# Twelve dummy matmuls and a fill of four in the head of a fused state-space and feed-forward layer, its four parameter vectors transposed together

## The chip, the cores and the metric

The kernel runs on one core of one Trainium2 chip. The metric is the device time of one execution in microseconds (us), lower is better. The time before is 183.56 us, the median of three runs (183.51 to 183.78).

## The reference, cut to what matters

```python
xn = _layernorm(x, axis=-1)              # x: (1, 2048, 512) bf16
# A: a diagonal state space model over 512 complex states
dt = jnp.exp(log_dt); Lam_bar = jnp.exp(dt * Lam)
B_bar = ((Lam_bar - 1.0) / Lam)[:, None] * Bmat
Bu = jnp.einsum("bld,pd->blp", xn + 0j, B_bar)
for t in range(L): h = Lam_bar * h + Bu[:, t, :]; hs.append(h)
A = 2.0 * jnp.einsum("blp,dp->bld", hseq, Cmat).real + xn * Dskip
# B: a gated feed-forward layer, F = 1376
B = (_silu(xn @ w_gate) * (xn @ w_up)) @ w_down
return x + A + B
```

Four parameter vectors of 512 numbers (`Lambda_re`, `Lambda_im`, `log_dt`, `Dskip`) steer part A.

## The kernel before, in words

The 2048 rows are 16 tiles of 128, worked in four chunks of 512 columns of the transposed input. Per chunk TensorE computes the gate and up projections (11 tiles of F each, `ffn_gate`, `ffn_up`, both by `ffn_mm`, L733), the projection into the state space (`ssm_b_chunk`, L814), the down projection (`dc_chunk`, L902) and the way back out of the states (L918). The scalar engine (ACT) evacuates PSUM and applies silu, the vector engine (DVE) normalizes, scans over time and adds up, GpSimd (POOL) computes a few powers. Results of TensorE go through eight PSUM banks; `next_bank` deals them in turn from a counter and passes over a bank that TensorE has written and for which no reader has been recorded yet. A matmul into a bank waits for the last reader of what the bank held.

Each step is recorded as a task with its reads and writes. TensorE's and the sync engine's tasks run in the order of recording; the tasks of DVE, ACT and POOL are ordered by a list scheduler from estimated times, and then run in that order, each engine by itself and strictly in turn.

The head, which the change touches, is recorded so:

- `pe_warm(9)` (L466): nine matmuls of 512 columns on a constant operand of ones. Their result is not used.
- `ln_head`: statistics and normalization of the first four tiles on DVE, with POOL for the reciprocal root (`rstd`). The normalized tile a is `xn0` to `xn3`.
- `ffn_gate_quarters` (L760): gate tiles 0 to 5 of the first chunk in quarters of 128 columns, so that each quarter can start when its row tile is transposed. Tiles 0 to 2 (A) need only the first weight load `ld_wgA`, tiles 3 to 5 (B) need `ld_wg0`. The transposes (L572) of row tile a are called `xT`a here and their evacuation by ACT (L578) `xTev`a. Between the first tile's transposes and its matmuls stands `pe_fill(3)` (L474): three dummies of 128 columns.
- `params_t` (L483, L486): the parameter vectors, loaded as rows by ACT's DMA queue, are transposed by TensorE and copied to SBUF by DVE: vectors 0 to 2 (`parT0`) after the first quarter, vector 3 (`Dskip`, `parT3`) before the last quarter. With vector 3 come four diagonal matrices `diagD` on DVE (L490).
- From the copied parameters POOL computes `dt` (L635), DVE `thn` (L637) and a row of small operations, ACT the phase table `tm0` (L684), DVE its reduction `tt1s0`, `tzs0` (L686, L688), ACT the sine table `sinT0` (L690). In ACT's order `xTev2`, `tm0`, `xTev3`, `tm1`, `sinT0` stand ahead of the six `silu` (L786) that evacuate the six gate tiles, `silu0_0` first.
- Then come the up projections of the same tiles, `mm_u0_0` to `mm_u0_5` (L733), and the rest of the kernel.

Of the kernel before, what the change touches and what calls it, by code (L numbers as in the profile page):

```python
# [18 lines left out]
    ffn_evac_act=(True, True, True, True),  # L19
    ln_norm_act=(False, False, True, True),  # L20
    wprep_act=True,
    warm=9,
    prio_tab=0.0,
    prio_par=0.0,
    rs_dve_from=8,
# [226 lines left out]
def bass_parallel_sum__ssm_conv_s5__swiglu_ffn__prompt_kernel(  # L252
# [30 lines left out]
    g = _Graph()  # L283
    es = ExitStack()
    with es:
# [53 lines left out]
        def one_c(n):  # L339
            return nc.const_aps.tensor(1.0, [128, n], B16)  # L340
# [19 lines left out]
        pbank = _PB()  # L360
# [15 lines left out]
        def next_bank():  # L376
            for _ in range(NB):
                b = bank_ctr[0] % NB
                bank_ctr[0] += 1
                if not _bank_live(b):  # L380
                    return b
            raise AssertionError("all PSUM banks live")
# [3 lines left out]
        def BK(b):  # L386
            return [("bk", b, 0), ("bk", b, 1)]
# [51 lines left out]
        def loads_stage_b2():  # L439
# [14 lines left out]
              writes=[("iot",)], name="iota", est=1000)  # L454
# [4 lines left out]
              name="act_warm", est=220, prio=1e6)  # L459

        def pe_warm(n):
            bk = next_bank()

            def mm(e, bk=bk):
                for _ in range(n):
                    inst = e.matmul(pbank[:, bk, :], lhsT=one_c(128), rhs=one_c(512), start=True, stop=True)  # L466
                return inst
            g.add("pe", mm, writes=BK(bk), name="pe_warm", est=n * 430, ninst=n)

        def pe_fill(n, bk):  # L470

            def mm(e, bk=bk):
                for _ in range(n):
                    inst = e.matmul(pbank[:, bk, 0:128], lhsT=one_c(128), rhs=one_c(128), start=True, stop=True)  # L474
                return inst
            g.add("pe", mm, writes=BK(bk), name="pe_warm_fill", est=n * 107, ninst=n)

        def params_t(ks):
            slot = next_tr()

            def tr(e, slot=slot):
                for k in ks:
                    inst = e.transpose(out=ptr[:, slot, 4 * k:4 * k + 4], in_=prow[0:4, k, :], identity=ident[0:4, 0:4])  # L483
                return inst
            g.add("pe", tr, reads=[("prow", k) for k in ks] + [("ident",)], writes=BK(slot), name="parT%d" % ks[0], est=30 * len(ks), ninst=len(ks))
            g.add("dve", lambda e, slot=slot: e.tensor_copy(out=praw[:, ks[0]:ks[-1] + 1].rearrange("p k a -> p (k a)"), in_=ptr[:, slot, 4 * ks[0]:4 * ks[-1] + 4]),  # L486
                  reads=BK(slot), writes=[("praw", k) for k in ks], name="parTev%d" % ks[0], est=80, prio=5000.0)
            if 3 in ks:
                for kt in range(KT):
                    g.add("dve", lambda e, kt=kt: e.tensor_scalar(out=diagD[:, kt, :], in0=ident[:], scalar1=praw[:, 3, kt:kt + 1], scalar2=None, op0=ALU.mult),  # L490
                          reads=[("praw", 3), ("ident",)], writes=[("diagD", kt)], name="diagD%d" % kt, est=90)
# [41 lines left out]
        def XN(c, j):  # L533
            return [("xnT", c % 2, j, 0), ("xnT", c % 2, j, 1)]
# [29 lines left out]
        def xt_tile_fine(c, a, parts=1):  # L564
            n = KT // parts
            for h in range(parts):
                slot = next_tr()
                k0 = h * n

                def tr(e, a=a, slot=slot, k0=k0):  # L570
                    for kt in range(k0, k0 + n):
                        inst = e.transpose(out=ptr[:, slot, (kt - k0) * 128:(kt - k0 + 1) * 128],  # L572
                                           in_=xn_sb[:, a % NXN, kt * 128:(kt + 1) * 128], identity=ident[:])
                    return inst
                g.add("pe", tr, reads=[("xn", a % NXN), ("ident",)], writes=BK(slot), name="xT%d_%d" % (a, h), est=n * 64, ninst=n)

                def evac(e, a=a, slot=slot, k0=k0):
                    return e.activation(out=xnT[:, c % 2, a % 4, k0:k0 + n, :],  # L578
                                        in_=ptr[:, slot, 0:n * 128].rearrange("p (k t) -> p k t", k=n), func=AF.Identity)
                g.add("act", evac, reads=BK(slot), writes=(XN(c, a % 4) if parts == 1 else [XN(c, a % 4)[h]]), name="xTev%d_%d" % (a, h), est=130 + 110 * n, prio=20000.0)  # L580
# [140 lines left out]
        def wres(nm, i):  # L721
            if nm == "wg" and i < 3:
                return ("wg", "a")
            return (nm, 0 if i < 6 else 1)
# [24 lines left out]
        def ffn_gate_quarters(c, tiles):  # L749
            xt_tile_fine(c, 4 * c, parts=2)  # L750
            banks = {i: next_bank() for i in tiles}

            def quarter(q, ts, h0, h1):
                for i in ts:
                    fs = fsz[i]
                    bk = banks[i]

                    def mm(e, bk=bk, i=i, fs=fs, q=q):
                        for kt in range(2 * h0, 2 * h1):
                            inst = e.matmul(pbank[0:fs, bk, q * 128:(q + 1) * 128], lhsT=wg[:, kt, i * 128:i * 128 + fs], rhs=xnT[:, c % 2, q, kt, :],  # L760
                                            start=(kt == 0), stop=(kt == KT - 1))
                        return inst
                    n = 2 * (h1 - h0)
                    g.add("pe", mm, reads=[wres("wg", i)] + XN(c, q)[h0:h1], writes=BK(bk), name="mm_gq%d_%d_%d_%d" % (c, i, q, h0), est=n * 62, ninst=n)

            A, B = tiles[:3], tiles[3:]
            pe_fill(3, banks[tiles[-1]])
            quarter(0, A, 0, 1)
            xt_tile_fine(c, 4 * c + 1)
            quarter(0, A, 1, 2)  # L770
            quarter(0, B, 0, 2)
            params_t([0, 1, 2])
            quarter(1, A, 0, 2)
            xt_tile_fine(c, 4 * c + 2)
            quarter(1, B, 0, 2)
            xt_tile_fine(c, 4 * c + 3)
            quarter(2, tiles, 0, 2)
            params_t([3])
            quarter(3, tiles, 0, 2)
            for i in tiles:  # L780
                fs = fsz[i]
                bk = banks[i]
                sl = gctr[0] % NG
                gctr[0] += 1
                sg_slot[(c, i)] = sl
                g.add("act", lambda e, sl=sl, bk=bk, fs=fs: e.activation(out=sg[0:fs, sl, :], in_=pbank[0:fs, bk, :], func=AF.Silu),  # L786
                      reads=BK(bk), writes=[("sg", sl)], name="silu%d_%d" % (c, i), est=490)
# [145 lines left out]
        if _CFG["warm"]:  # L933
            pe_warm(_CFG["warm"])
        ln_head()
        ffn_gate_quarters(0, [0, 1, 2, 3, 4, 5])
        params_a()
        tables()
# [98 lines left out]
```

## Time and profile before

| what | value |
|---|---|
| median of the runs | 183.56 us (183.51 to 183.78) |
| profiled execution | 184.87 us |
| its span, first to last instruction | 183.1 us |
| TensorE busy in the span | 179.2 us (98%), 939 matmuls |
| DVE busy | 166.2 us (91%) |
| ACT busy | 92.2 us (50%) |
| POOL busy | 13.1 us (7%) |
| TensorE in the chain that ended last | 95% |

The profile is one execution. The chain that ended last is followed back from the last instruction, at each step to what released it. In the timeline each row has a start, a length, an engine, a line of the kernel, the operation with what it writes and reads, and a count; in brackets stands how long the engine had been idle and what ended that. A matmul row's length ends with its last matmul's drain, so that matmuls in a stream start closer together than one lasts.

### The profile page before, as it was taken

The page shows a single profiled execution, that of the slowest core. Times are in us where ns is not written, and L with a number is a line of the kernel's source. Part 1 is how long each engine was busy: PE and PEld are TensorE (multiplying, and loading weights), DVE is VectorE, ACT ScalarE, POOL GpSimd, SP SyncE. Part 2 cuts the span into 40 slices and gives each one's busy share as a digit, 9 for nine tenths or more (in the row PEclk, how much of TensorE's full clock was granted, in tenths as well). Part 3 has the DMA queues.
Part 4 walks back from the last instruction along what each step waited for, and adds up shares of the span by engine and source line. Part 5 has one row for each costly group of instructions (what it writes and reads, how often), then busy time and mean ns, then how long its engine had stood idle before and what let it go on. Part 6 is the DMA issues. An engine that isn't in the chain of part 4 may idle for free.

```text
span 183.1 us, 2586 instructions
## 1 busy us (share of the span) xinstructions
PE 179.2 (98%) x939; PEld 88.5 (48%) x939; DVE 166.2 (91%) x360; ACT 92.2 (50%) x163; POOL 13.1 (7%) x29
## 2 busy tenths in 40 slices
PE   8899999999999999999999999999999999999994
PEld 2795444444444545444444554444444444444643
DVE  3668898999999998999999989999999999999963
ACT  3259999997799407147667471017766630000000
POOL 4340220000000005000000050000000000000000
PEclk9999999999999999999999999999999999999999
DMA  5993467669200000630000000620000000000202
GB/s 135 321 378 88 91 119 115 141 182 352 72 0 4 0 0 0 116 118 0 0 0 0 0 4 0 115 87 27 0 4 2 2 0 0 0 32 0 82 32 86
DMA packets 23404, 12.39 MB, mean 68 GB/s; under 512 B 15104, under 2 KB 23392, under 8 KB 23392
## 3 DMA queue, kind: packets, MB, share of 16 engines
q1 hardware_dynamic: 23360, 12.23, 24.7%
q8 instruction: 7, 0.11, 0.3%
q14 instruction: 5, 0.04, 0.1%
q10 hardware_dynamic: 32, 0.00, 0.0%
HBM read 6.46 MB, written 2.10 MB: 47 GB/s over the span
## 4 chain that ended last, share of the span: by engine, by line
PE 95%; DMA 2%; SPq 1%; DVE 0%; issue 0%
PE pb L733 39%; PE pb L902 21%; PE pb L918 15%; PE pb L814 15%; PE pb L760 4%; DMA wg<-in_B_w_gate_dram 2%; PE pb L905 1%; SPq L406 1%; PE pb L572 0%; DVE osb L929 0%; PE pb L483 0%
## 5 line engine op out<-in xcount | busy, mean ns | idle before, releaser
L733 PE MATMUL pb<-xnT,wu 128*128 128x512 bf16 (+1 forms) x176 | 43.7, 379 | 0.0
L902 PE MATMUL pb<-wd,hT 128*128 128x512 bf16 (+3 forms) x187 | 39.7, 367 | 0.0
L853 DVE TENSOR_TENSOR_SCAN vq<-sm,car,vq 128x512 bf16<-128x512 f32 x32 | 39.5, 1270 | 0.1
L733 PE MATMUL pb<-xnT,wg 128*128 128x512 bf16 (+1 forms) x152 | 38.4, 379 | 0.0
L798 ACT ACTIVATE uf<-pb 128x512 bf16<-128x512 f32 (+1 forms) x44 | 25.9, 605 | 17.4 <-DVE hT L800 10.2
L918 PE MATMUL pb<-W,hss 128*128 128x512 bf16 (+1 forms) x136 | 28.3, 366 | 0.0
L814 PE MATMUL pb<-xnT,BT 128*128 128x512 bf16 x128 | 28.1, 379 | 0.0
L733 PEld LDWEIGHTS pb<-xnT,wu 128*128 128x128 bf16 (+1 forms) x176 | 17.6, 100 | 20.1
L902 PEld LDWEIGHTS pb<-wd,hT 128*128 128x128 bf16 (+1 forms) x187 | 18.0, 98 | 18.5
L746 ACT ACTIVATE sg<-pb 128x512 bf16<-128x512 f32 (+1 forms) x38 | 22.6, 597 | 7.2 <-PE pb L733 6.9
L733 PEld LDWEIGHTS pb<-xnT,wg 128*128 128x128 bf16 (+1 forms) x152 | 15.3, 101 | 17.6
L800 DVE TENSOR_TENSOR hT<-sg,uf 128x512 bf16<-128x512 bf16 (+1 forms) x44 | 18.5, 420 | 2.9 <-ACT uf L798 1.2
L918 PEld LDWEIGHTS pb<-W,hss 128*128 128x128 bf16 x136 | 13.2, 98 | 13.9
L821 ACT ACTIVATE u_sb<-pb 128x512 bf16<-128x512 f32 x16 | 9.6, 597 | 20.4 <-PE pb L814 19.8
L814 PEld LDWEIGHTS pb<-xnT,BT 128*128 128x128 bf16 x128 | 12.5, 98 | 15.1
L505 POOL TENSOR_TENSOR rstd<-ve,mhalf 128x1 f32<-128x1 f32 x16 | 9.6, 618 | 92.5 <-DVE ve L503 92.5
L499 DVE BATCH_NORM_STATS2 st<-x_sb 128x6 f32<-128x512 bf16 x16 | 10.2, 681 | 2.9 <-DMA x_sb<-in_A_x_dram 2.9
L859 DVE TENSOR_TENSOR scrA<-vq,cosT 128x1024 bf16<-128x1024 bf16 x16 | 10.9, 684 | 0.0
L863 DVE TENSOR_TENSOR scrA<-vq,sin 128x1024 bf16<-128x1024 bf16 x16 | 10.9, 683 | 0.0
L847 DVE TENSOR_TENSOR scrA<-u_sb,sin 128x1024 bf16<-128x1024 bf16 x16 | 10.9, 682 | 0.0
L844 DVE TENSOR_TENSOR scrA<-u_sb,cosT 128x1024 bf16<-128x1024 bf16 x16 | 10.9, 680 | 0.0
L823 ACT ACTIVATE u_sb<-pb 128x512 bf16<-128x512 f32 x16 | 9.5, 593 | 2.3 <-PE pb L814 2.3
(72 smaller groups left out, 136.2 us busy)
## 6 DMA issues: line engine op xcount, KB each, us to landing
out_dram<-osb SPq DMA_DIRECT2D x15, 128.0 KB, 1.7
x_sb<-in_A_x_dram SPq DMA_DIRECT2D x3, 512.0 KB, 7.4
wd<-in_B_w_down_dram SPq DMA_DIRECT2D x1, 1280.0 KB, 6.9
wg<-in_B_w_gate_dram SPq DMA_DIRECT2D x2, 384.0 KB, 4.2
wu<-in_B_w_up_dram SPq DMA_DIRECT2D x1, 768.0 KB, 6.9
wg<-in_B_w_gate_dram SPq DMA_DIRECT2D x1, 608.0 KB, 8.0
wu<-in_B_w_up_dram SPq DMA_DIRECT2D x1, 608.0 KB, 9.1
x_sb<-in_A_x_dram SPq DMA_DIRECT2D x4, 128.0 KB, 2.2
```

What stands on the lines that cost most here:

```text
L733: inst = e.matmul(pbank[0:fs, bk, :].rearrange("p (j t) -> p j t", j=4), lhsT=w[:, kt, i * 128:i * 128 + fs], rhs=xnT[:, c % 2, :, kt, :], ...
L746: g.add("act", lambda e, sl=sl, bk=bk, fs=fs: e.activation(out=sg[0:fs, sl, :], in_=pbank[0:fs, bk, :], func=AF.Silu), reads=BK(bk), write ...
L798: g.add("act", lambda e, ul=ul, bk=bk, fs=fs: e.activation(out=uf[0:fs, ul, :], in_=pbank[0:fs, bk, :], func=AF.Identity), reads=BK(bk), w ...
L800: g.add("dve", lambda e, sl=sl, ul=ul, fs=fs, i=i, hb=hb: e.tensor_tensor(out=hT[0:fs, hb, i, :], in0=sg[0:fs, sl, :], in1=uf[0:fs, ul, :] ...
L814: inst = e.matmul(pbank[:, bk, :].rearrange("p (j t) -> p j t", j=4), lhsT=BT[:, ri, kt, pt * 128:(pt + 1) * 128], rhs=xnT[:, c % 2, :, kt ...
L844: g.add("dve", lambda e, sl=sl, U=U, Cb=Cb: e.tensor_tensor(out=pr2[:, sl, 0], in0=U, in1=Cb, op=ALU.mult), reads=ru + rdt, writes=[("pr", ...
L847: g.add("dve", lambda e, sl=sl, Usw=Usw, S2=S2: e.tensor_tensor(out=pr2[:, sl, 1], in0=Usw, in1=S2, op=ALU.mult), reads=ru + rdt, writes=[ ...
L853: g.add("dve", lambda e, sl=sl, ri=ri, pt=pt, rr=rr, c=c: e.tensor_tensor_scan(out=vq[:, sl, 1, ri, :], data0=rr[:, pt:pt + 1].to_broadcas ...
L859: g.add("dve", lambda e, sl=sl, Q=Q, Cb=Cb: e.tensor_tensor(out=po2[:, sl, 0], in0=Q, in1=Cb, op=ALU.mult), reads=rq + rdt, writes=[("po", ...
L863: g.add("dve", lambda e, sl=sl, Qsw=Qsw, S2sw=S2sw: e.tensor_tensor(out=po2[:, sl, 1], in0=Qsw, in1=S2sw, op=ALU.mult), reads=rq + rdt, wr ...
L902: inst = e.matmul(pbank[:, bk, 0:nc_], lhsT=hT[0:fs, hb, i, lt * 128:(lt + 1) * 128], rhs=wd[0:fs, i, c0:c0 + nc_], start=(i == 0), stop=F ...
L918: inst = e.matmul(pbank[:, bk, 0:nc_], lhsT=hss[:, hb, pt, ri, lt * 128:(lt + 1) * 128], rhs=W12[:, ri, pt, c0:c0 + nc_], start=False, sto ...
```

## The change

The stream of dummies at the start grows from nine matmuls of 512 columns to ten, and two of 128 columns follow. The fill between the first transposes and the first gate matmuls grows from three to four. The four parameter vectors are transposed in one step, where vectors 0 to 2 stood, and copied in one step; the later step for vector 3 is gone. With that one call of `next_bank` goes too, so that the banks behind it are dealt differently, and the scheduler places the `diagD` behind `xn3`.

```diff
-    warm=9,
+    warm=10,
...
                 for _ in range(n):
                     inst = e.matmul(pbank[:, bk, :], lhsT=one_c(128), rhs=one_c(512), start=True, stop=True)
+                for _ in range(2):
+                    inst = e.matmul(pbank[:, bk, 0:128], lhsT=one_c(128), rhs=one_c(128), start=True, stop=True)
                 return inst
-            g.add("pe", mm, writes=BK(bk), name="pe_warm", est=n * 430, ninst=n)
+            g.add("pe", mm, writes=BK(bk), name="pe_warm", est=n * 430 + 220, ninst=n + 2)
...
-            pe_fill(3, banks[tiles[-1]])
+            pe_fill(4, banks[tiles[-1]])
             quarter(0, A, 0, 1)
             xt_tile_fine(c, 4 * c + 1)
             quarter(0, A, 1, 2)
             quarter(0, B, 0, 2)
-            params_t([0, 1, 2])
+            params_t([0, 1, 2, 3])
             quarter(1, A, 0, 2)
             xt_tile_fine(c, 4 * c + 2)
             quarter(1, B, 0, 2)
             xt_tile_fine(c, 4 * c + 3)
             quarter(2, tiles, 0, 2)
-            params_t([3])
             quarter(3, tiles, 0, 2)
```

## The prediction, made before the changed kernel ran

> **What bounds the kernel now.** I read the chain of waits first, then the timeline of TensorE over the first 17 us, then the timeline of the other engines there. The chain, in order of time (start, us, what):
>
> ```profile
> 2.18 3.99 DMA wg<-in_B_w_gate_dram
> 6.17 0.14 issue
> 6.30 0.80 PE pb L760 x6
> ...
> 13.15 0.11 PE pb L483
> 13.26 1.45 PE pb L760 x24
> 14.70 13.81 PE pb L733 x64
> ```
>
> A load of gate weights (`ld_wgA`) lands at 6.17; from 6.30 on TensorE is the path without a break until the last tile at 180.66. The list of waits has only two for TensorE, 0.8 us at the start and 0.4 us before the first transposes, both in the head. Going through the code's dependencies with the trace's times, every later matmul group has its operands and its bank at least 5 us early, but two: `mm_b2_0_0` (0.42 us after its transposing DMA landed, which TensorE itself releases, so it moves along) and `mm_b3_0_0` (2.2 us, the same way). A us won or lost before `mm_u0_0` (the first L733, at 14.54) is therefore a us of the whole. The prediction is the new start of `mm_u0_0`.
>
> The head on TensorE (start, length, then line and count):
>
> ```profile
> 0.82 4.00 PE L466 MATMUL pb<-const-bfloat16-1.0 128*128 128x512 bf16 x9 [0.82 <-PEq L1022]
> 5.26 0.58 PE L572 MATMUL pb<-ident,xn_sb 128*128 128x128 bf16 x4 [0.44 <-DVE ve L503]
> 5.64 0.52 PE L474 MATMUL pb<-const-bfloat16-1.0 128*128 128x128 bf16 x3
> 6.30 0.80 PE L760 MATMUL pb<-xnT,wg 128*128 128x128 bf16 x6
> 6.90 0.63 PE L572 MATMUL pb<-ident,xn_sb 128*128 128x128 bf16 x4
> 7.32 2.13 PE L760 MATMUL pb<-xnT,wg 128*128 128x128 bf16 x18
> 9.38 0.23 PE L483 MATMUL pb<-ident,prow 4*128 4x4 bf16 x3
> ...
> 11.65 1.50 PE L760 MATMUL pb<-xnT,wg 128*128 128x128 bf16 x24
> 13.08 0.17 PE L483 MATMUL pb<-ident,prow 4*128 4x4 bf16 x1
> ```
>
> The same 128-column matmul comes every (2.13 - 0.31)/17 = 107 ns at 7.3 us and every (1.50 - 0.22)/23 = 56 ns at 11.7 us (0.31 and 0.22 are the length of one). The spacing changes at 10.2 us in the trace. The page's clock row shows full speed throughout, so the spacing is what must be read: TensorE runs at half rate to 10.2 us. Nine dummies at 0.427 us did not raise it; it rose 3.9 us after TensorE's last pause, the one before 6.30.
>
> The vector and scalar engines just before the gate tiles are evacuated:
>
> ```profile
> 9.66 0.17 DVE L486 COPY praw<-pb 128x12 bf16<-128x12 bf16 x1 [1.68 <-PE pb L483]
> 9.90 1.11 POOL L635 TENSOR_TENSOR sm<-ecst,praw 128x4 f32<-128x4 f32 x1 [1.52 <-DVE praw L486]
> 11.05 0.16 DVE L637 SCALAR_TENSOR_TENSOR sm<-sm,praw 128x4 f32<-128x4 f32 x1 [0.83 <-POOL sm L635]
> 12.49 0.40 DVE L686 TENSOR_SCALAR scrC<-scrC 128x512 f32<-128x512 f32 x1
> 12.92 0.69 DVE L688 SCALAR_TENSOR_TENSOR scrC<-scrC 128x512 f32<-128x512 f32 x1
> 13.65 0.63 ACT L690 ACTIVATE sin<-scrC 128x512 bf16<-128x512 f32 x1 [0.39 <-DVE scrC L688]
> 14.18 3.02 ACT L786 ACTIVATE sg<-pb 128x512 bf16<-128x512 f32 x6
> ```
>
> This second chain starts at the parameter transposes and ends in the six `silu`, which stand behind `sinT0` in ACT's queue. In the kernel before it ends just off the path: `silu0_0` finishes at 14.76 and `mm_u0_1`, which takes its bank, starts at 15.40.
>
> **The change, part by part.**
>
> *Dummies.* A tenth dummy and two short ones follow 4.19 (the ninth's start): 4.62 + 0.43 + 2 x 0.107 = 5.26, where the transposes start anyway on `xn0` (done 5.11). A fourth fill ends at 5.64 + 4 x 0.107 = 6.07, before 6.30. Cost nothing; their cover is the wait for `xn0` and for `ld_wgA`, and if either came early the dummies would cost at most 0.65 and 0.1 us. What they change is the pauses: 0.65 + 0.34 us without a running matmul (4.62 to 5.26, 5.96 to 6.30) become 0.23 us (6.07 to 6.30). By the one rise in the trace, 3.9 us after the last long pause, the clock would rise at 0.82 + 3.9 = 4.7 us; if the pause at 6.1 still spoils it, at 10.2 as now. I take the early rise. Anywhere before about 7 us gives the same sum, since the next limit is at 7.6.
>
> Against the early rise could speak that four transposes fall into that stretch. The trace's stretch before 10.2 holds four transposes (6.90), three small ones (9.38) and a 0.14 us gap, and the clock rose behind it, so by this row they don't prevent it. The Trainium skill (TensorE: Matmul & The Clock Gate, Part 4) says that transposes do not count as busy for this clock; by that the stretch with the dummies might fail as well, which is the second rival's time, 183.86.
>
> *What the faster clock meets.* The six matmuls and transposes after 6.30 speed up, but `quarter(0, B)` needs `ld_wg0`, landed at 7.59: start 7.59 + 0.14 (as behind `ld_wgA`) = 7.73. Before it was 7.96. Then at 56 ns: 12 matmuls, last one starts at 8.35; four parameter transposes (the first 0.15 behind it as at 13.08, then 0.046, 0.027, 0.027 as at 9.38), last start 8.61. Then 0.09 + 12 x 0.056 + 4 x 0.056 + 12 x 0.056 + 4 x 0.056 brings `quarter(2)` to 10.48, just when `xTev2` is done; 24 matmuls to 11.82 (`xTev3`, behind `tm0` on ACT, is done near 11.65); without the second parameter transpose (0.2 us around 13.08) 24 more to 13.16. If nothing else bound, `mm_u0_0` would start 14.54 - 13.16 = 1.38 us earlier.
>
> *The bank.* Here the joined transposes cost something. `next_bank` deals eight banks in turn. Before, `parT3` took the bank after `xT3`'s, and the counter wrapped past the six live gate banks so that `mm_u0_0` got `xT3`'s bank, free since 12.65, and `mm_u0_1` the bank of gate tile 0. Without `parT3`, `mm_u0_0` gets the bank of gate tile 0 and must wait for `silu0_0`. So the second chain becomes the path, and everything behind `mm_u0_0` in TensorE's queue waits with it. Its new times, each step by the offsets of the rows above:
> - last parameter transpose 8.61, copy 0.20 later: 8.81; POOL's `dt` 0.24 later: 9.05; `thn` 1.15 later: 10.19.
> - `thn` to `tt1s0`: 1.44 (11 small operations); the new order swaps a reciprocal for a cast, 0 to 0.1 less: 11.54 to 11.64. `tm0` on ACT, from 10.45 to 11.16, is in time.
> - `tzs0` 0.43 later, `sinT0` 0.73 after that, `silu0_0` 0.54 after that and 0.58 long: 13.82 to 13.92. `mm_u0_0` 0.10 later: 13.92 to 14.02.
>
> I take 13.97: TensorE stands idle from 13.16 to 13.97, and 14.54 - 13.97 = 0.57 us are left of the 1.38. `mm_u0_1` needs `silu0_1` 0.49 us later, while `mm_u0_0` lasts 0.86: no second wait.
>
> *diagD and the copy.* The four `diagD` move from 13.72 up behind `xn3`. They take 0.74 us (0.25 each, 0.16 apart), into the 0.83 us in which the vector engine waits for `dt`: nothing, with 0.1 to 0.25 us of room; without that cover up to 0.74. The second copy (0.15) goes. The fourth parameter vector has landed at 4.04.
>
> **Sum.** Profiled execution: 184.87 us, of which the span is 183.1; less 0.57 is 184.3. The median of the runs is 1.31 below the profiled execution; I carry the difference over: 183.56 - 0.57 = 182.99. What a measurement of this kernel can tell from no change is about 0.2%, 0.37 us, so the gain is only just above it.
>
> **Rivals.**
>
> *The clock is early already in the timed runs (slower).* The nine dummies run 3.8 us without a pause, and the rise in the trace came 3.9 us after one: a hair decides. The profiled execution is 1.31 us over the median. Were the clock full by 6.3 us in the timed runs of the kernel before, its `mm_u0_0` would start at 13.16 + 0.20 (the second transpose is still there) = 13.36, 1.18 earlier than in the profile, which is nearly that 1.31. Then the change brings only the bank wait: 13.97 - 13.36 = +0.61, 184.17. It decides once the clock rises before about 8 us without the change. Against it: profiling may lengthen a run by itself, and the three runs lie within 0.27 us. The Trainium skill (TensorE: Matmul & The Clock Gate, Part 1) says that the window runs freely and does not restart with the kernel, so the rise would differ from run to run; the trace has one execution and can't show it.
>
> *The dummies don't raise the clock.* The pause at 6.07, or operands that are all ones, spoil it, and the rise stays at 10.2. Then the second chain starts only 0.03 us later than before and loses 0 to 0.1 on the way: `mm_u0_0` at 14.79 to 14.89, +0.25 to +0.35, 183.86.
>
> *No bank wait.* If the chain to `silu0_0` ran ahead of what I add up, the limit is 13.16: 182.18. Every row of that chain speaks against it.
>
> *The new pause of 0.8 us drops the clock again.* Half a rate over another 3.9 us, the time the rise took, would cost 3.9/2 = 1.95 us more: about 184.9. For it: pauses of 1.0 us in all kept the clock down before 6.3 us. Against it: once risen, it is not seen to fall in this trace, which has no such pause behind the rise.
>
> **How the numbers follow.** Forecast 0.48; early already, or early in some runs, 0.27; clock not raised 0.14; no bank wait 0.04; clock drops 0.07. Faster by over 0.2%: four fifths of the forecast, and the 0.04: 0.42. Slower: four fifths of 0.27, the 0.07 and some of the unraised clock (its upper bound is at the edge): 0.34. The rest within: 0.24. The forecast's own range is 182.75 to 183.25 (0.25 us for the unknown order of small operations and the landings). The range for 8 in 10 takes in the early case: 182.7 to 184.25.
>
> **What would show it.** Spacing of L762 (the old L760) at 56 ns from 6.8 us or earlier, `quarter(0, B)` at 7.7; the copy of the parameters near 8.8 with one width of 16; the four `diagD` before `thn`; TensorE idle for about 0.8 us before the first L735, released by ACT; that line at 13.9 to 14.0. Wrong if 107 ns lasts to 10.2 (dummies do nothing), if no idle stands before the first up-projection (no bank wait), or if the profile shows 0.6 gained and the timed runs don't (the clock differed between them).

## The result and the profile after

The changed kernel is slower: 184.06 us median of 10 runs (183.86 to 184.71) against 183.53 us of 10 runs of the kernel before (183.25 to 183.83), ratio 1.0033, 95% interval 1.0019 to 1.0047. Yet the two profiled executions stand the other way: the span is 182.5 us after and was 183.1 us before. The profiled execution lies 0.25 us above the median of the runs after (184.31 us), and lay 1.34 us above it before (184.87 us). Both comparisons are true, and why they differ is the point of what follows.

The chain that ended last, after (start, us, what; the longest pieces):

```profile
3.19 4.50 DMA wg<-in_B_w_gate_dram
7.74 0.84 PE pb L762 x12
9.05 1.12 POOL sm L637
11.96 0.70 DVE scrC L690
12.68 0.63 ACT sin L692
13.31 0.49 ACT sg L787
13.94 13.97 PE pb L735 x64
```

TensorE is no longer the path from 6.3 us on. The path leaves it after `quarter(0, B)` and the four parameter transposes behind it (L485), goes over POOL, the vector and the scalar engine to the first silu (L787) and comes back at 13.94. The list of TensorE's waits says the same:

```profile
PE pb L466 <- PEq L1023: 0.8, 1, 0.8
PE pb L735 <- ACT sg L787: 0.6, 1, 0.6
PE pb L762 <- DMA wg<-in_B_w_gate_dram: 0.3, 1, 0.3
```

TensorE's timeline in the head:

```profile
0.82 4.42 PE L466 MATMUL pb<-const-bfloat16-1.0 128*128 128x512 bf16 x10 [0.82 <-PEq L1023]
5.04 0.42 PE L468 MATMUL pb<-const-bfloat16-1.0 128*128 128x128 bf16 x2
5.25 0.63 PE L574 MATMUL pb<-ident,xn_sb 128*128 128x128 bf16 x4
...
6.37 0.49 PE L762 MATMUL pb<-xnT,wg 128*128 128x128 bf16 x6
...
7.74 0.84 PE L762 MATMUL pb<-xnT,wg 128*128 128x128 bf16 x12 [0.31 <-DMA wg<-in_B_w_gate_dram]
8.51 0.25 PE L485 MATMUL pb<-ident,prow 4*128 4x4 bf16 x4
...
10.49 2.84 PE L762 MATMUL pb<-xnT,wg 128*128 128x128 bf16 x48
13.94 4.26 PE L735 MATMUL pb<-xnT,wu 128*128 128x512 bf16 x19 [0.61 <-ACT sg L787]
```

The dummies run into the transposes without a pause, as forecast, and six matmuls take 0.49 us at 6.37 where they took 0.80: the clock record in the trace, which lists from when to when TensorE was granted which rate, has the full rate from 6.37 us on (before: from 10.21). The time at which the full rate begins is called the rise from here on. Three rows of the chain to the silu:

```profile
8.80 0.17 DVE L488 COPY praw<-pb 128x16 bf16<-128x16 bf16 x1 [0.76 <-PE pb L485]
...
10.19 0.17 DVE L639 SCALAR_TENSOR_TENSOR sm<-sm,praw 128x4 f32<-128x4 f32 x1 [0.25 <-POOL sm L637]
...
13.22 3.02 ACT L787 ACTIVATE sg<-pb 128x512 bf16<-128x512 f32 x6
```

Added up in the prediction: copy 8.81, `thn` 10.19, `silu0_0` from 13.24 to 13.34, `mm_u0_0` at 13.97. Measured: 8.80, 10.19, 13.22, 13.94. The profile of the changed kernel is the forecast one. What was not forecast is how the timed runs stand to the first profile.

### The profile page after: what moved, and what is told of

The parts are those of the page before. It is cut to its first block, busy times and chain, and to the rows that moved or that the text cites. A ratio compares the mean times of both kernels' runs of the same rounds, so it can differ in the third digit from the quotient of the medians.

```text
span 182.5 us, 2586 instructions
## 1 busy us (share of the span) xinstructions
PE 177.8 (97%) x935; PEld 87.4 (48%) x943; DVE 165.9 (91%) x359; ACT 92.5 (51%) x163; POOL 13.1 (7%) x29
## 4 chain that ended last, share of the span: by engine, by line
PE 91%; DMA 2%; DVE 2%; SPq 1%; issue 1%; ACT 1%; POOL 1%
PE pb L735 39%; PE pb L903 21%; PE pb L815 15%; PE pb L919 15%; DMA wg<-in_B_w_gate_dram 2%; SPq L406 1%; PE pb L906 1%; POOL sm L637 1%; PE pb L762 0%; DVE scrC L690 0%; ACT sin L692 0%; ACT sg L787 0%; DVE osb L930 0%; DVE sm L611 0%; DVE scrC L688 0%
## 5 line engine op out<-in xcount | busy, mean ns | idle before, releaser
L903 PE MATMUL pb<-wd,hT 128*128 128x512 bf16 (+3 forms) x181 | 38.9, 366 | 0.3
```

What stands on the lines that cost most here:

```text
L903: inst = e.matmul(pbank[:, bk, 0:nc_], lhsT=hT[0:fs, hb, i, lt * 128:(lt + 1) * 128], rhs=wd[0:fs, i, c0:c0 + nc_], start=(i == 0), stop=F ...
```

## The experiments

Theory A: the time at which TensorE's clock rises differs from execution to execution. In most executions of the kernel before, nine dummies bring the rise before the first gate matmul; the first profile caught one of the others. Then the change has nothing to win with its dummies in the median, and pays the bank wait. Theory B: the clock rises at about 10 us in all executions of the kernel before, and the profiled one was longer for another reason. First, four kernels on one chip, which share 35 runs of the kernel before (183.51 us median).

**A second profile of the kernel before.** No edit.

> The kernel before, unchanged, for a second profile. Theory A (the clock is up early in the timed runs of the kernel before, and the first profile caught an execution in which it was late): most executions have a span near 181.8 us (183.53 less the 1.77 that lie around the span); a profile of such a one shows 128-column matmuls 56 ns apart from 6.3 us on and the first up-projection at 13.3 to 13.4. Theory B (the clock is late in all executions, the profiled one is longer for another reason): 107 ns up to about 10 us and the first up-projection near 14.5 again. Time 183.5 either way.

Measured: 183.55 us, ratio 0.9995 (0.9978 to 1.0013), spans of the 12 runs from 181.5 to 182.1 us. Its timeline:

```profile
0.82 4.00 PE L466 MATMUL pb<-const-bfloat16-1.0 128*128 128x512 bf16 x9 [0.82 <-PEq L1022]
5.34 0.50 PE L572 MATMUL pb<-ident,xn_sb 128*128 128x128 bf16 x4 [0.52 <-DVE ve L503]
...
6.29 0.50 PE L760 MATMUL pb<-xnT,wg 128*128 128x128 bf16 x6 [0.28 <-DMA wg<-in_B_w_gate_dram]
...
7.63 0.84 PE L760 MATMUL pb<-xnT,wg 128*128 128x128 bf16 x12 [0.29 <-DMA wg<-in_B_w_gate_dram]
...
13.25 4.05 PE L733 MATMUL pb<-xnT,wu 128*128 128x512 bf16 x18
```

The same program, the same dummies, but the six matmuls at 6.29 take 0.50 us (0.80 in the first profile) and the up-projection starts at 13.25 instead of 14.54, 1.29 us earlier; the spans differ by as much (181.8 and 183.1). The clock's record has the rise at 5.62 us here, and the profiled execution (183.59 us) lies 0.04 us above the median of its runs, so that it is not the profiling that lengthens an execution by 1.3 us. Theory B is out. In the kernel before, the pause between dummies and transposes (0.52 us by this profile) did not prevent the rise.

**The dummies alone.**

```diff
-            params_t([0, 1, 2, 3])
+            params_t([0, 1, 2])
...
             quarter(2, tiles, 0, 2)
+            params_t([3])
```
(against the changed kernel)

> The dummies alone (ten and two, then four), the parameter vectors transposed in two steps as before. Theory A: nothing left to win, 183.5 (-0.1 to +0.1). Theory B: the whole 1.2 us of the earlier clock without the bank wait, 182.35.

Measured: 183.54 us, ratio 0.9996 (0.9972 to 1.0020). Nothing to win, as theory A has it; its rise was at 4.65 us.

**The joined transposes alone** (`warm=9`, `pe_fill(3)`, no short dummies):

> The joined transposes alone, nine dummies and a fill of three as before. Theory A: the bank wait at full price, 13.97 instead of 13.36 for the first up-projection, +0.6: 184.1, the same as the whole change. Theory B: the chain to the first silu is late by itself, +0.25 to +0.35: 183.85.

Measured: 184.12 us, ratio 1.0032 (1.0012 to 1.0052). This part alone is as slow as the whole change.

**The whole change with the bank given back:**

```diff
             quarter(2, tiles, 0, 2)
+            next_bank()
             quarter(3, tiles, 0, 2)
```

> The whole change with one bank dealt and left unused where the second parameter transpose stood, so that the first up-projection gets the bank it had before. Theory A: the wait for the first silu goes, the removed transpose step is won: 13.16 against 13.36, -0.2: 183.3. Theory B: -1.38: 182.15. If the wait has another cause than the bank: 184.06 as in the changed kernel.

Measured: 183.18 us, ratio 0.9983 (0.9966 to 0.9999). One call that computes nothing takes 0.88 us off the changed kernel. This version and the joined transposes alone happen to start `quarter(0, B)`, which waits for `ld_wg0`, at the same time in their profiles, so that these can be laid side by side. First the joined transposes alone, then the version with the spare bank:

```profile
7.32 0.84 PE L760 MATMUL pb<-xnT,wg 128*128 128x128 bf16 x12 [0.25 <-DMA wg<-in_B_w_gate_dram]
...
13.52 3.83 PE L733 MATMUL pb<-xnT,wu 128*128 128x512 bf16 x17 [0.60 <-ACT sg L785]
```

```profile
7.32 0.84 PE L762 MATMUL pb<-xnT,wg 128*128 128x128 bf16 x12 [0.31 <-DMA wg<-in_B_w_gate_dram]
...
12.76 4.48 PE L735 MATMUL pb<-xnT,wu 128*128 128x512 bf16 x20
```

From the same 7.32 the up-projection comes 13.52 - 12.76 = 0.76 us later where it waits for the silu: that is the price of the bank.

Four more kernels, on another chip with 31 runs of the kernel before (183.52 us median), ask what holds the bank, what the dummies are worth, and whether more can be won.

**Two silu ahead of the sine table.** Banks as in the changed kernel; the tasks `sinT0` and `msinT0` get the additional order

```diff
+                      order=((silu_q[0], silu_q[1]) if pt == 0 else ())
```

> The whole change, banks dealt as in it, but on ACT the first two silu go ahead of the first sine table. If the wait before the first up-projection is for the bank of gate tile 0 and that bank is held up by the sine table ahead of it in ACT's order, the first silu ends near 13.0 instead of 13.8 and the wait goes: the first up-projection at 13.1 to 13.3, 183.2 to 183.4, like the version with the spare bank. If the bank is not what holds it, 184.06 as in the changed kernel.

Measured: 183.35 us, ratio 0.9986 (0.9970 to 1.0002); 0.7 us below the changed kernel, though `mm_u0_0` still takes the bank of gate tile 0. ACT, then TensorE, from its timeline:

```profile
12.17 3.02 ACT L789 ACTIVATE sg<-pb 128x512 bf16<-128x512 f32 x6
```

```profile
13.04 4.26 PE L735 MATMUL pb<-xnT,wu 128*128 128x512 bf16 x19
```

The silu start at 12.17 instead of 13.22, and no idle time stands before the up-projection. The added order names two silu; the scheduler put all six ahead, and the first sine table went from 12.68 to 16.46. So it is the bank, and the bank is held by ACT's order.

**No dummies at all.** `pe_warm` only takes its bank, `pe_fill` is gone, the rest as before the change.

> The kernel before without any dummies, its banks dealt as before. If the clock needs a stretch of about 3.4 us that TensorE works almost through, and such stretches lie differently in every execution, the rise comes between 8.5 and 12 us in all of them, and the first up-projection between 13.7 and 15.4: 183.9 to 185.6, median near 184.7, a wide spread. If the dummies do nothing for the timed runs (the clock is up at their start for another reason), 183.5 as before.

Measured: 184.98 us (184.34 to 185.75, 8 runs), ratio 1.0072 (1.0045 to 1.0100). Its profile has the rise at 10.22 us and the up-projection at 14.46, as in the first profile of the kernel before:

```profile
6.16 0.80 PE L755 MATMUL pb<-xnT,wg 128*128 128x128 bf16 x6 [0.35 <-ACT xnT L573]
...
14.46 2.75 PE L728 MATMUL pb<-xnT,wu 128*128 128x512 bf16 x12
```

The level is 0.3 us above what I expected, the spread of 1.4 us as expected.

**The spare bank with nine dummies** (the version with the spare bank, `warm=9`, `pe_fill(3)`, no short ones):

> The joined transposes with the spare bank, nine dummies and a fill of three as before. If the new dummies win nothing in most executions: median 183.2 as with them, and about one execution in nine near 184.4 (late clock, as 4 of 35 of the kernel before had a span of 183.1 us or more). If the new dummies carry the gain of the version with the spare bank: 183.5.

Measured: 183.34 us, ratio 0.9990 (0.9970 to 1.0009), one of 12 runs at 184.51. The median lies 0.16 above the version with the new dummies, which these runs can't tell from nothing. The late executions can be counted among those with a mean granted clock of 0.999 or more. With nine dummies (kernel before, its copy, the joined transposes with and without the spare bank) 6 of 109 executions are 1.1 us or more above their kernel's median; with the twelve and four (changed kernel, dummies alone, spare bank, silu first, and the next one) none of 58. Three more runs of the kernel before, at 185.13, 185.60 and 186.59 us, are not counted: their mean granted clock is 0.991, and the 0.9% lost are 1.65 us by themselves. So in about one execution of eighteen the new dummies may do what they were added for. This is suggested, not shown: at one in eighteen, 58 executions without a late one have a chance of about 4 in 100, none of the late ones was profiled, and the dummies alone had two executions 0.77 and 0.83 us above their median.

**Parameters transposed during the wait for `ld_wg0`** (on the version with the spare bank):

```diff
+            params_t([0, 1, 2, 3])
             quarter(0, B, 0, 2)
-            params_t([0, 1, 2, 3])
```

> The version with the spare bank, and the four parameter transposes ahead of the first quarter of gate tiles 3 to 5, into the 0.3 us in which TensorE waits for the load of their weights. They cost TensorE nothing there: first up-projection 0.3 us earlier, 182.9. If the vector engine, which now takes the parameters' copy before the last statistics, makes the third or fourth row tile late, the gain is lost: 183.2 or more.

Measured: 183.32 us, ratio 0.9979 (0.9961 to 0.9997), not the 182.9 hoped for. The transposes do fall into the gap (7.18), but a new wait takes most of the gain. ACT, then TensorE, from its timeline:

```profile
8.99 0.72 ACT L686 ACTIVATE scrC<-iot,sm 128x512 f32<-128x512 f32 x1 [1.44 <-DVE sm L639]
9.62 0.58 ACT L580 ACTIVATE xnT<-pb 128x512 bf16<-128x512 bf16 x1
```

```profile
9.81 0.39 PE L574 MATMUL pb<-ident,xn_sb 128*128 128x128 bf16 x4
10.25 2.85 PE L762 MATMUL pb<-xnT,wg 128*128 128x128 bf16 x48
```

The scheduler now puts `tm0` (L686) ahead of `xTev2` (L580) on ACT, which so ends at 10.20, and the third quarter waits for it: it starts 0.44 us after the transposes in front of it, where it starts 0.23 us after them in the version with the spare bank. No idle time stands in TensorE's row, since the transposes' drain reaches to 10.20. From the start of `quarter(0, B)` to the up-projection it is 5.37 us (7.57 to 12.94), against 5.44 with the spare bank alone. I had looked for the loss on the vector engine; it came on ACT.

## Why the prediction was wrong

- **The bank wait: right, and the path of the change.** 13.97 forecast, 13.94 measured. Its price was put at 0.81 us (13.16 to 13.97); the two profiles with the same start have 0.76.
- **The dummies: right in what they do to an execution with a late clock.** The pauses shrank as worked out, and the rise came at 6.37 us. In the five profiles with twelve dummies it came between 3.80 and 6.37 us. The rule behind it was wrong: the one rise in the first trace, 3.9 us after a pause, was taken for a fixed delay that gives 4.7 us. The prediction says itself that any rise before about 7 us gives the same sum, so this cost nothing here.
- **Between the two profiled executions the sum holds:** -0.57 forecast, -0.6 in the spans.
- **The step that failed is in the sum's last line: "The median of the runs is 1.31 below the profiled execution; I carry the difference over".** That 1.31 was no constant that lies between a profile and its runs but the late clock itself: the second profile has the up-projection 1.29 us earlier. Of the timed runs the spans of the kernel before are mostly 181.4 to 182.1, and time less span is 1.77 in the first profile (184.87 - 183.1) as in the second (183.59 - 181.8 = 1.79). A gain that only an execution with a late clock can have was thus taken off a median that is not made by such executions: the dummies alone measured 183.54 against 183.51.
- **The first rival is what happened.** Put at 0.61 and 184.17; measured +0.53 and 184.06. In its terms: bank wait 0.76, less 0.18 for the removed transpose step, is 0.58. (From the start of `quarter(0, B)` to the up-projection it is 5.62 us in the second profile and 5.44 with the spare bank; the runs of the nine-dummy version with the spare bank also lie 0.18 below the kernel before, which their interval can't tell from nothing.) The stated range of 182.7 to 184.25 holds 184.06 because it was drawn to take in this rival, not because the forecast was near. The near equality of 1.18 and 1.31 had been seen and was given a chance of 0.27, behind the carried difference. The Trainium skill (TensorE: Matmul & The Clock Gate, Part 1) says that the window over which this clock is decided runs freely and does not start with the kernel. This case's profiles agree: with the same nine dummies the rise came at 10.21, 5.62, 4.70 and 4.28 us.
- **The other rivals fell:** the clock was raised by the dummies, the wait was there, and no clock drop followed the 0.8 us pause in the changed kernel's profile (matmuls of 512 columns stay 0.22 us apart behind it).
- **diagD and the copy: right.** The `diagD` ran from 9.21 to 9.95, inside the wait for `dt`, which left 0.25 us of idle time.

## What to carry to other kernels

Before a gain is taken off a median, ask whether the profiled execution is a typical one: its time against the timed runs tells, and a difference as large as the stall that is to be removed is a warning that most executions don't have the stall. A call that only deals a buffer is part of the schedule: when a step with its buffer goes, look up which release each step behind it now waits for, and where that release stands in its engine's order. Here a spare bank, or the silu ahead of a sine table, gave back 0.7 to 0.9 us.

## What the runs showed of the hardware

The rise of TensorE's clock is a matter of the execution, not of the program alone: 10.21 and 5.62 us in two profiles of the kernel before, and 4.70 and 4.28 us in the two other kernels with the same dummies. Without dummies the runs spread over 1.4 us; with nine most lie within 0.6 us and a few 1.1 us or more above; with twelve there was none of these.

A stretch need not be worked through without pause: the second profile of the kernel before rose at 5.62 us although TensorE had started nothing between the end of the last dummy's stream at 4.62 and the transposes at 5.34. Nor did transposes keep the clock down: four of them began at 5.34, just ahead of this rise.

The ten traces allow a reading of what decides, which no run here tested. Their records of the full rate last 174.08 or 177.49 us, which is 51 or 52 times 3.413 us. Counted back from the rise in steps of 3.41 us, the stretch that ends at the rise holds at most 0.72 us without a running stream of matmuls, and every earlier one at least 0.85. In the second profile of the kernel before, the stretch from 2.21 to 5.62 has one pause, of 0.72 us. In the first, the stretch up to 3.39 has the 0.85 us up to the first dummy, and the next, up to 6.80, has both pauses, 0.98 us together; so the rise came one stretch later, at 10.21. By this reading it is where the stretches lie against the kernel's start that makes an execution late, and the new dummies help by closing the second of these stretches. In the changed kernel's profile the one from 2.96 to 6.37 has 0.26 us of pause; with the pauses of the first profile it would have 0.98 (an estimate).

By the clock row on the profile's page all these executions ran at full speed (mean 1.00), since the clock record begins with the first rise; the half rate before it shows only in the spacing of the matmuls. What brought the mean granted clock of three runs of the kernel before down to 0.991 was not looked into.
